# Tail keys and last queries as 64-row matmuls, one double bank for both heads' outputs, and FFN on two banks

## The chip, the core and the metric

The kernel runs on one core of a Trainium2 chip. The metric is the device time of one execution in microseconds (us); the kernel before has a median of 394.3 us over 3 runs (393.31 to 398.42). A separate execution was recorded by the hardware profiler, and every time of a single instruction comes from that one. Engines are named as in the profile: PE (TensorE, matmuls) with PEld (its weight loads), DVE (VectorE), ACT (ScalarE), POOL (GpSimd) and SP (SyncE, which issues DMAs). PE writes its results to PSUM, eight banks of 512 fp32 values per partition.

## The reference

Attention with a relative-position bias over 8 batches, 8 heads, 576 positions and 64 dimensions, then a feed-forward network (FFN) on the 4608 tokens that come out:

```python
scores = scale * np.matmul(q, k.transpose(0, 1, 3, 2))
bias = bias_table[bucket]            # bucket depends on |i - j| alone, constant from 128 on
scores = scores + bias.transpose(2, 0, 1)[None, :, :, :]
attn = np.exp(scores - np.max(scores, axis=-1, keepdims=True))
attn = attn / (np.sum(attn, axis=-1, keepdims=True) + 1e-09)
x = np.matmul(attn, v)               # transposed and reshaped to 4608 x 512
h = x @ w_in                         # 512 -> 2048
g = np.maximum(0.01 * h, h)
out = g @ w_out                      # 2048 -> 512
```

## The kernel before

**Head pairs.** Work goes by head pair: 8 batches of 4 pairs make 32 items, and the main loop has 33 passes. Pass n computes the scores of pair n and the value product of pair n-1. The program writes the order of every engine out by hand; each engine executes its instructions in that order and waits only on semaphores.

**Scores.** For a pair, the transposed keys `kt` and queries `qt` hold head 0 in partitions 0 to 63 and head 1 in partitions 64 to 127. 576 = 4 x 128 + 64, so there are four blocks of 128 keys and a tail of 64 keys, and likewise 512 queries and a last 64. `qk_mm(n, u)` makes one piece of the scores, transposed (keys in partitions). For u = 0 to 3 it is a key block against the first 512 queries, one 64-row matmul for each head (L301). For u = 4 it is the four key blocks against the last 64 queries (L305): these are 128-row matmuls, for which `apart` (L278) has made a copy of the last queries of both heads, side by side, with the other head's rows zeroed. For u = 5 it is the tail keys of both heads, masked by `apart` in the same way, against all queries (L308, L309). Scores go to `ps_s`, two buffers of two banks each.

**Exp and bias.** ACT takes the exp of each piece into `at_` or `at4_` (L319, L321, L326). DVE multiplies the band near the diagonal by the exp of the bias (`band`, L344).

**Value product.** `av(n, e)` makes head e's output in `ps_o`, which has a single bank: for each of five blocks of queries, four matmuls over the key blocks (L357) and one over the tail keys (L359). The tail matmul has 128 rows, with the other head's half of `v4` set to zero. A column of ones beside v gives the row sum; DVE takes its reciprocal and multiplies into `opair` (L362, L363). `x_transposes` then turns `opair` into `xT`, on PE for the first pairs and the last one and by a DMA on SP for the others.

**Queries and keys.** `transpose_q` and `transpose_k` for pair n+1 run within pass n. For the first ten pairs PE transposes (L272), and a copy takes the result out of PSUM (L286 on ACT or DVE, L291 on DVE); later a DMA on SP turns them ahead of time, and DVE copies from `tu`.

**FFN pieces.** A tile of 512 tokens is 16 "in" pieces (`ffn_in`: four matmuls into one bank, then ACT's Prelu, L393 and L395) and 16 "out" pieces (`ffn_out`: four of the sixteen matmuls into one bank, L404, and after every fourth piece DVE's copy to `y`, L409, and a store on SP). There are nine tiles. `moe(k)` puts k pieces at its place in a pass; `choose` picks "in" or "out" from counters that the program keeps while it is built: a tile's "in" pieces may start once its tokens are `ready` and not more than two tiles are open. A pass has seven such places for eight pieces in all. What is left over runs in `moe_rest` behind the last pass. FFN pieces and PE's transposes share `ps_m`, three buffers of one bank. With `ps_s` (four) and `ps_o` (one) this fills the eight banks.

**Around it.** `spin` runs matmuls on a tile of zeros while the first loads arrive. Loads of q, k and v are issued on POOL; transposing DMAs and output stores on SP.

Of the kernel before, what the change touches and what calls it, by code (L numbers as in the profile page):

```python
# [37 lines left out]
def kernel(  # L38
# [17 lines left out]
    P = 128  # L56
# [23 lines left out]
    ps_m_pool = ctx.enter_context(tc.tile_pool(name="ps_m", bufs=3, space=bass.MemoryType.PSUM))  # L80
# [18 lines left out]
    v4 = [per.tile([P, n_pairs, 2, D + 1], BF16, name=f"v4_{i}") for i in range(NBUF)]  # L99
# [16 lines left out]
    def load_v_part(b, j):  # L116
        i = b % NBUF
        for c in ((0,), (1, 2), (3,))[j]:
            nc.gpsimd.dma_start(  # L119
                out=vn[i][:, c, :, 0:D],  # L120
                in_=v[b, :, c * P : (c + 1) * P, :].rearrange("h s d -> s h d"),
            )
        if j == 2:
            for e in range(2):
                nc.gpsimd.dma_start(
                    out=v4[i][e * SL : (e + 1) * SL, :, e, 0:D],
                    in_=v[b, e::2, NJ * P : S, :].rearrange("h s d -> s h d"),
                )

    def load_v(b, h0, h1, by_head):  # L130
        i = b % NBUF
        p0, p1 = h0 // 2, h1 // 2
        if by_head:
            for h in range(h0, h1):
                nc.gpsimd.dma_start(
                    out=vn[i][:, :, h, 0:D],
                    in_=v[b, h, 0 : NJ * P, :].rearrange("(c s) d -> s c d", s=P),
                )
        else:
            for c in range(NJ):  # L140
                nc.gpsimd.dma_start(
                    out=vn[i][:, c, h0:h1, 0:D],
                    in_=v[b, h0:h1, c * P : (c + 1) * P, :].rearrange("h s d -> s h d"),
                )
        for e in range(2):
            nc.gpsimd.dma_start(
                out=v4[i][e * SL : (e + 1) * SL, p0:p1, e, 0:D],
                in_=v[b, h0 + e : h1 : 2, NJ * P : S, :].rearrange("h s d -> s h d"),
            )

    def clear_v(eng, i):
        eng.memset(v4[i], 0.0)
        for e in range(2):
            eng.memset(v4[i][e * SL : (e + 1) * SL, :, e, D : D + 1], 1.0)
        eng.memset(vn[i][:, :, :, D : D + 1], 1.0)
# [110 lines left out]
    def turned_pair(n, j):  # L266
# [3 lines left out]
        ps = ps_m_pool.tile([P, 8 * P], BF16, name="ps_t", tag="m")  # L270
# [12 lines left out]
    def transpose_q(n):  # L283
        qt = qts[n] = qt_pool.tile([P, S + P], BF16, name="qt")
        copy = nc.scalar.copy if n <= n_pairs and n != 1 else nc.vector.tensor_copy
        copy(out=qt[:, 0:S].rearrange("p (r c) -> p r c", c=NC), in_=turned_pair(n, 0))  # L286
        apart(qt)
# [6 lines left out]
    def qk_mm(n, u):  # L294

        qt, kt = qts[n], kts[n]
        ps = ps_s_pool.tile([P, 2, 512], FP32, name="ps_s")
# [5 lines left out]
        elif u == NJ:  # L303
            for c in range(NJ):
                nc.tensor.matmul(ps[:, 0, c * P : (c + 1) * P], lhsT=kt[:, c * P : (c + 1) * P],  # L305
                                 rhs=qt[:, S : S + P], start=True, stop=True)
# [8 lines left out]
    def exp_band(n, u, ps):  # L315
        b, p = items[n]
# [3 lines left out]
        elif u == NJ:  # L320
            nc.scalar.activation(  # L321
                at[:, :, :, 512:S].rearrange("p e c i -> p c e i"),
                ps[:, 0, :].rearrange("p (c e i) -> p c e i", e=2, i=SL),
                AF.Exp, scale=scale)
        else:
            nc.scalar.activation(at4[:, 0:S], ps.rearrange("p e i -> p (e i)")[:, 0:S], AF.Exp, scale=scale)  # L326
        if n > 1:
            band(n, u)
# [16 lines left out]

    def av(n, e):
        b, p = items[n]
        i = b % NBUF
        at, at4 = at_[n % 2], at4_[n % 2]
        if e == 0:  # L350
            ops_[n] = op_pool.tile([P, NJ + 1, 2 * D], BF16, name="opair")
        opair = ops_[n]
        ps = ps_o_pool.tile([P, NJ + 1, D + 1], FP32, name="ps_o", tag="ps_o")
        for ic in range(NJ + 1):
            for c in range(NJ):
                o = (e * NJ + c) * S + ic * P
                nc.tensor.matmul(ps[:, ic, :], lhsT=at[:, o : o + P], rhs=vn[i][:, c, 2 * p + e, :],  # L357
                                 start=(c == 0), stop=False)
            nc.tensor.matmul(ps[:, ic, :], lhsT=at4[:, ic * P : (ic + 1) * P], rhs=v4[i][:, p, e, :],  # L359
                             start=False, stop=True)  # L360
# [24 lines left out]
    gts = {}  # L385

    def ffn_in(T):
        t0 = T * TT
        gt = gts[T] = gt_pool.tile([P, n_fc, TT], BF16, name="gt")
        for f in range(n_fc):  # L390
            pm = ps_m_pool.tile([P, TT], FP32, name="pm1", tag="m")
# [6 lines left out]
    def ffn_out(T):  # L398
        t0 = T * TT
        gt = gts.pop(T)  # L400
        for ts in range(TT // P):
            pm = ps_m_pool.tile([P, DM], FP32, name="pm2", tag="m")
# [14 lines left out]
    turn = 0  # L417
# [31 lines left out]
    def moe(n_pieces):  # L449
        nonlocal turn  # L450
        for _ in range(n_pieces):
            kind = choose()
            turn ^= 1

            if kind and not (kind == "out" and made["in"] == 1 and running["in"] is None and turn):
                piece(kind)

    def moe_rest():
        while (kind := choose()):
# [9 lines left out]
    pw = ps_o_pool.tile([P, 512], FP32, name="ps_w", tag="ps_o")  # L469

    def spin(k):
        for _ in range(k):
# [12 lines left out]
    for n in range(N + 1):  # L485
        live = n < N
        if live:
            b, p = items[n]
            if n == 0:
                load_w_in(0)  # L490
                load_v(1, 0, H, False)
                load_w_in(1)
                load_w_out(0)
                load_w_out(1)
            elif 0 < b < B - 1:
                if p < 2:
                    load_qk(b + 1, 4 * p, 4 * p + 4)
                if p > 0:
                    load_v_part(b + 1, p - 1)
            if n + 1 < N and not by_dma(n + 1):  # L500
                pair_rows(n + 1)
            if n + AHEAD < N and by_dma(n + AHEAD):
                pair_rows(n + AHEAD)
                turn_by_dma(n + AHEAD)
            ps_a, ps_b = qk_mm(n, 0), qk_mm(n, 1)
            exp_band(n, 0, ps_a)
        moe(1)
        if live:
            exp_band(n, 1, ps_b)
        if n > 1:  # L510
            av(n - 1, 0)
        if n + 1 < N:
            transpose_q(n + 1)
        if n < 2:
            spin(3)
        moe(1)
        if live:
            ps_a, ps_b = qk_mm(n, 2), qk_mm(n, 3)
            exp_band(n, 2, ps_a)
        moe(1)  # L520
        if n > 1 and x_by_dma(n - 2):
            finished(n - 2)
        if live:
            exp_band(n, 3, ps_b)
        if n > 1:
            av(n - 1, 1)
        if n + 1 < N:
            transpose_k(n + 1)
        if n == 0:
            spin(4)  # L530
        if n == 1:
            spin(3)
        moe(1)
        if live:
            ps_a, ps_b = qk_mm(n, 4), qk_mm(n, 5)
            exp_band(n, 4, ps_a)
        if n == 1:
            exp_band(1, 5, ps_b)

            bands(0)  # L540
            av(0, 0)
            av(0, 1)
        moe(1)
        if n > 0:
            x_transposes(n - 1)
            if not x_by_dma(n - 1):
                finished(n - 1)
        moe(1)
        if n == 1:
            bands(1)  # L550
        elif live:
            exp_band(n, 5, ps_b)
# [32 lines left out]
```

## Time and profile before

| what | value |
|---|---|
| timed runs, median (lowest to highest) | 394.3 us (393.31 to 398.42) |
| span of the profiled execution, first to last instruction | 435.3 us |
| granted TensorE clock in it | 0.852 |
| PE busy | 421.2 us, 97% of the span |
| PEld, DVE, ACT, POOL busy | 199.4, 209.3, 242.2, 69.0 us |
| first FFN matmul at | 41.53 us |

The profiled execution has no other time of its own than its span. It is longer than the timed runs, and its durations on PE go with the clock granted there. PE's busy time is modelled and counts overlapping matmuls once, so the distance between the starts of matmuls tells more than their printed lengths. A row of the timeline gives the start, the length in us, the engine, the line, the tiles written and read, and the number of instructions merged.

### The profile page before, as it was taken

What the parts mean: (1) busy time and instruction counts of PE and PEld (TensorE: products, weight loads), DVE (VectorE), ACT (ScalarE), POOL (GpSimd) and SP (SyncE); (2) the same over time, 40 slices, a digit from 0 to 9 for tenths busy, and PEclk for the clock granted to TensorE, in tenths of its full rate; (3) what the DMA queues carried; (4) which work ended last, traced back from release to release, by engine and by line L of the source; (5) the groups of instructions that cost most, each with busy time, mean ns of one, the idle gap of its engine ahead of it and who ended that gap; (6) DMA issues with size and microseconds to landing.
All of it is one profiled execution on the core that took longest, in us unless ns stands there. A gap on an engine that the chain in (4) does not pass through costs nothing.

```text
span 435.3 us, 8219 instructions
## 1 busy us (share of the span) xinstructions
PE 421.2 (97%) x3384; PEld 199.4 (46%) x3384; DVE 209.3 (48%) x551; ACT 242.2 (56%) x343; POOL 69.0 (16%) x100
## 2 busy tenths in 40 slices
PE   8777999999999999999999999999999999999996
PEld 3445555444444444444444444444444454444442
DVE  6588557764556455555555455545554320000111
ACT  4776776576645666476646764676457713354000
POOL 8834230420051002400060004000000000000000
PEclk9888888888888888888888888888888888888888
DMA  8999992999289714974399349522422010000111
GB/s 107 194 196 197 206 168 42 106 131 146 64 82 172 113 27 81 185 123 44 68 152 171 44 68 98 115 37 54 60 65 17 24 43 24 26 24 0 74 48 72
DMA packets 103613, 39.89 MB, mean 92 GB/s; under 512 B 82576, under 2 KB 97944, under 8 KB 103576
## 3 DMA queue, kind: packets, MB, share of 16 engines
q0 software_dynamic: 53664, 18.36, 40.5%
q1 hardware_dynamic: 49912, 21.02, 26.8%
q8 instruction: 26, 0.43, 0.4%
q14 instruction: 11, 0.09, 0.1%
HBM read 37.68 MB, written 9.45 MB: 108 GB/s over the span
## 4 chain that ended last, share of the span: by engine, by line
PE 91%; DVE 5%; ACT 2%; issue 1%; ACTq 0%
PE ps_o L357 9%; PE ps_s L301 7%; PE ps_o L359 2%; PE ps_w L473 2%; PE ps_s L305 2%; PE ps_s L308 2%; DVE opair L363 1%; DVE at_113 L344 1%; PE pm_2157 L404 1%; PE pm_4504 L404 1%; PE pm_3930 L404 1%; PE pm_1566 L404 1%; PE pm_3339 L404 1%; PE pm_2748 L404 1%; PE pm_3191 L404 1%
## 5 line engine op out<-in xcount | busy, mean ns | idle before, releaser
L393 PEld LDWEIGHTS <-w_in_sb 128*128 128x128 bf16 x576 | 55.9, 104 | 75.6 <-issue 8.3
L404 PEld LDWEIGHTS <-gt 128*128 128x128 bf16 x576 | 54.2, 104 | 78.1 <-issue 15.0
L319 ACT ACTIVATE at_114<-ps_s 128x1024 bf16<-128x1024 f32 x64 | 62.9, 1023 | 29.4 <-PE ps_s L301 29.2
L319 ACT ACTIVATE at_113<-ps_s 128x1024 bf16<-128x1024 f32 x64 | 62.6, 1022 | 14.3 <-PE ps_s L301 14.1
L344 DVE TENSOR_TENSOR at_114<-at_114,hk 128x512 bf16<-128x512 bf16 (+1 forms) x64 | 32.2, 506 | 38.4 <-ACT at_114 L319 30.1
L344 DVE TENSOR_TENSOR at_113<-at_113,hk 128x512 bf16<-128x512 bf16 (+1 forms) x64 | 32.0, 506 | 37.9 <-ACT at_113 L319 33.7
L357 PEld LDWEIGHTS <-at_114 128*128 128x128 bf16 x640 | 29.4, 100 | 12.9 <-DVE opair L363 3.1
L357 PEld LDWEIGHTS <-at_113 128*128 128x128 bf16 x640 | 28.9, 100 | 12.6 <-DVE opair L363 3.9
L363 DVE TENSOR_TENSOR opair<-ps_o,rcp 128x320 bf16<-128x320 f32 x64 | 31.5, 491 | 2.2
L119 POOL DMA_DIRECT2D vn_107<-in_v_dram x12 | 10.7, 907 | 99.0 <-PE ps_o L359 98.9
L119 POOL DMA_DIRECT2D vn_106<-in_v_dram x12 | 10.6, 892 | 83.9 <-PE ps_o L359 79.5
L301 PE MATMUL ps_s<-qt,kt_111 64*128 64x512 bf16 x128 | 21.4, 405 | 1.0 <-ACT at_113 L321 0.4
L301 PE MATMUL ps_s<-qt,kt_110 64*128 64x512 bf16 x128 | 21.1, 403 | 0.7 <-ACT at_113 L319 0.5
L362 DVE RECIPROCAL rcp<-ps_o 128x5 f32<-128x5 f32 x64 | 12.2, 190 | 17.0 <-PE ps_o L359 17.0
L357 PE MATMUL ps_o<-vn_106,at_114 128*128 128x65 bf16 x320 | 15.7, 198 | 2.2 <-DVE opair L363 1.5
L357 PE MATMUL ps_o<-vn_106,at_113 128*128 128x65 bf16 x320 | 15.5, 198 | 2.3 <-DVE opair L363 2.1
L359 PEld LDWEIGHTS <-at_1_116 128*128 128x128 bf16 x160 | 15.9, 99 | 0.0
L359 PEld LDWEIGHTS <-at_0_115 128*128 128x128 bf16 x160 | 15.9, 99 | 0.0
L357 PE MATMUL ps_o<-vn_107,at_114 128*128 128x65 bf16 x320 | 15.2, 198 | 0.3 <-DVE opair L363 0.3
L357 PE MATMUL ps_o<-vn_107,at_113 128*128 128x65 bf16 x320 | 15.2, 198 | 0.2 <-DVE opair L363 0.2
L321 ACT ACTIVATE at_113<-ps_s 128x512 bf16<-128x512 f32 x16 | 9.5, 595 | 10.4 <-PE ps_s L305 10.4
L286 DVE COPY qt<-tu 128x576 bf16<-128x576 bf16 x22 | 14.2, 647 | 0.0
(879 smaller groups left out, 824.0 us busy)
## 6 DMA issues: line engine op xcount, KB each, us to landing
out_dram<-y SPq DMA_DIRECT2D x36, 256.0 KB, 2.2
w_in_sb<-in_moe_w_in_dram POOLq DMA_DIRECT2D x2, 1024.0 KB, 13.7
vn_107<-in_v_dram POOLq DMA_DIRECT2D x16, 128.0 KB, 5.7
w_out_sb<-in_moe_w_out_dram POOLq DMA_DIRECT2D x2, 1024.0 KB, 16.4
qn_102<-in_q_dram POOLq DMA_DIRECT2D x6, 288.0 KB, 12.5
kn_104<-in_k_dram POOLq DMA_DIRECT2D x6, 288.0 KB, 14.4
qn_103<-in_q_dram POOLq DMA_DIRECT2D x6, 288.0 KB, 7.4
kn_105<-in_k_dram POOLq DMA_DIRECT2D x6, 288.0 KB, 9.5
```

Of the source, the lines that this page charges most:

```text
L119: nc.gpsimd.dma_start(out=vn[i][:, c, :, 0:D], in_=v[b, :, c * P : (c + 1) * P, :].rearrange("h s d -> s h d"),)
L286: copy(out=qt[:, 0:S].rearrange("p (r c) -> p r c", c=NC), in_=turned_pair(n, 0))
L301: nc.tensor.matmul(ps[:, e, :], lhsT=kt[r, u * P : (u + 1) * P], rhs=qt[r, 0:512], start=True, stop=True)
L319: nc.scalar.activation(at[:, :, u, 0:512], ps, AF.Exp, scale=scale)
L321: nc.scalar.activation(at[:, :, :, 512:S].rearrange("p e c i -> p c e i"), ps[:, 0, :].rearrange("p (c e i) -> p c e i", e=2, i=SL), AF.Ex ...
L344: nc.vector.tensor_tensor(out=o, in0=o, in1=m, op=ALU.mult)
L357: nc.tensor.matmul(ps[:, ic, :], lhsT=at[:, o : o + P], rhs=vn[i][:, c, 2 * p + e, :], start=(c == 0), stop=False)
L359: nc.tensor.matmul(ps[:, ic, :], lhsT=at4[:, ic * P : (ic + 1) * P], rhs=v4[i][:, p, e, :], start=False, stop=True)
L362: nc.vector.reciprocal(rcp, ps[:, :, D : D + 1])
L363: nc.vector.tensor_tensor(out=opair[:, :, e * D : (e + 1) * D], in0=ps[:, :, 0:D], in1=rcp.to_broadcast([P, NJ + 1, D]), op=ALU.mult)
L393: nc.tensor.matmul(pm, lhsT=w_in_sb[:, c, f * P : (f + 1) * P], rhs=xT[c][:, t0 : t0 + TT], start=(c == 0), stop=(c == n_cc - 1))
L404: nc.tensor.matmul(pm, lhsT=gt[:, f, ts * P : (ts + 1) * P], rhs=w_out_sb[:, f, :], start=(f == 0), stop=(f == n_fc - 1))
```

## The change

- The tail keys' value product becomes ten 64-row matmuls for a pair (`av_tails`): head e uses partitions 64e to 64e+63 of `at4_` and `v4`, and no zeroed half is needed. It stands directly behind the first score visit.
- The last queries' scores (u = 4) become eight 64-row matmuls, head e into its own bank, behind u = 2 and 3. Queries no longer need `apart`.
- `ps_o` becomes one buffer of two banks, one for each head. The buffer is shared in turn with the scores of u = 4 (`ps_q`) and with PE's transposes of pairs 5 to 9 (`ps_tt`, q and k in one tile).
- `ps_m` has two buffers. Behind the last pass (`rest`), FFN takes banks from all three pools.
- The pass is put in another order: u = 0, 1, tails and head 0's output together, an "in" piece, head 1's output, an "in" piece, u = 2, 3, 4, a block of four pieces of one kind with u = 5 in its middle, two "in" pieces. `moe` places "in" pieces only; "out" pieces have their place only in the block. The copies for pair n+1 stand behind u = 5 from pass 4 on.
- The first two passes are written out ahead of the loop.

```diff
-    ps_m_pool = ctx.enter_context(tc.tile_pool(name="ps_m", bufs=3, space=bass.MemoryType.PSUM))
+    ps_m_pool = ctx.enter_context(tc.tile_pool(name="ps_m", bufs=2, space=bass.MemoryType.PSUM))
...
-        ps = ps_m_pool.tile([P, 8 * P], BF16, name="ps_t", tag="m")
+        if n <= n_pairs:
+            ps = ps_m_pool.tile([P, 8 * P], BF16, name="ps_t", tag="m")
+        else:
+            if j == 0:
+                turned[n] = ps_o_pool.tile([P, 2, 8 * P], BF16, name="ps_tt", tag="o")
+            ps = turned[n][:, j, :]
...
+        if u == NJ:
+            ps = ps_o_pool.tile([P, 2, 512], FP32, name="ps_q", tag="o")
+            for c in range(NJ):
+                for e in range(2):
+                    r = slice(e * D, (e + 1) * D)
+                    nc.tensor.matmul(ps[:, e, c * SL : (c + 1) * SL], lhsT=kt[r, c * P : (c + 1) * P],
+                                     rhs=qt[r, 512:S], start=True, stop=True)
+            return ps
...
-        elif u == NJ:
-            for c in range(NJ):
-                nc.tensor.matmul(ps[:, 0, c * P : (c + 1) * P], lhsT=kt[:, c * P : (c + 1) * P],
-                                 rhs=qt[:, S : S + P], start=True, stop=True)
...
+    def av_tails(n):
...
+        ps = outs[n] = ps_o_pool.tile([P, 2, 512], FP32, name="ps_o", tag="o")
+        for ic in range(NJ + 1):
+            for e in range(2):
+                r = slice(e * SL, (e + 1) * SL)
+                nc.tensor.matmul(ps[:, e, ic * (D + 1) : (ic + 1) * (D + 1)],
+                                 lhsT=at4[r, ic * P : (ic + 1) * P], rhs=v4[b % NBUF][r, p, :],
+                                 start=(ic == 0), stop=False)
...
     def moe(n_pieces):
...
+            if can("in"):
+                piece("in")
+
+    def moe_block():
+
+        kind = "out" if can("out") else "in"
+        for i in range(4):
+            if can(kind):
+                piece(kind)
+            if i == 1:
+                yield
+        yield
...
+    for n in range(2, N + 1):
         live = n < N
+        early = n + 1 <= n_pairs
+        if x_by_dma(n - 2):
+            finished(n - 2)
         if live:
...
+            begin(n)
             ps_a, ps_b = qk_mm(n, 0), qk_mm(n, 1)
+            exp(n, 0, ps_a)
+            exp(n, 1, ps_b)
+        av_tails(n - 1)
+        av(n - 1, 0)
+        if live:
+            band(n, 0)
+        if early:
+            transpose_q(n + 1)
+        moe(1)
+        av(n - 1, 1)
+        if live:
+            band(n, 1)
+        if early:
+            transpose_k(n + 1)
         moe(1)
         if live:
...
+            ps_a, ps_b, ps_c = qk_mm(n, 2), qk_mm(n, 3), qk_mm(n, 4)
+            exp(n, 2, ps_a)
+            band(n, 2)
+            exp(n, 3, ps_b)
+            exp(n, 4, ps_c)
+            band(n, 4)
+        x_transposes(n - 1)
+        if not x_by_dma(n - 1):
+            finished(n - 1)
+        block = moe_block()
+        next(block)
+        if live:
+            ps_a = qk_mm(n, 5)
+            exp(n, 5, ps_a)
+            band(n, 5)
+        if n + 1 < N and not early:
             transpose_q(n + 1)
+            transpose_k(n + 1)
+        next(block)
         moe(2)
     moe_rest()
```

More of the change, by code (lines that the diff above doesn't have):

```diff
@@ L416 @@
     share = 0
-    turn = 0
     def can(kind):
@@ L543 @@
[L543 to L552, printed above, removed]
+            ps_a, ps_b, ps_c = qk_mm(n, 2), qk_mm(n, 3), qk_mm(n, 4)
+            exp(n, 2, ps_a)
+            band(n, 2)
+            exp(n, 3, ps_b)
+            exp(n, 4, ps_c)
+            band(n, 4)
+        x_transposes(n - 1)
+        if not x_by_dma(n - 1):
+            finished(n - 1)
```

147 lines of the change are left out of this document (64 added, 83 removed).

## The prediction

> **What bounds the kernel now.** The page comes first: engine sums and granted clock; then the view of cores, and of the timeline the first FFN matmul.
>
> ```profile
> span 435.3 us, 8219 instructions
> PE 421.2 (97%) x3384; PEld 199.4 (46%) x3384; DVE 209.3 (48%) x551; ACT 242.2 (56%) x343; POOL 69.0 (16%) x100
> PEclk9888888888888888888888888888888888888888
> core 0: 435.3 us, clock 0.852
> ...
> 41.53 0.40 PE L393 MATMUL pm_780<-xT_94,w_in_sb 128*128 128x512 bf16 x1
> ```
>
> TensorE (PE) is the bound: every microsecond it idles or spends lands in the end, while DVE and ACT are half used. The profiled execution ran at clock 0.852, and its span alone is 41.0 us over the timed median of 394.3, so the timed runs had a faster clock. FFN work begins 41.5 us in; scaling the 393.8 us behind it by 0.852 gives 335.5, with the 41.5 before it 377, which leaves 17 us around the span. So I take the timed runs to be at about full clock, do the sum at the profile's clock first, and then once more with TensorE's times multiplied by 0.852 and DVE's and ACT's left alone.
>
> Next, the timeline over one steady pass (a head pair), cut to its turning points.
>
> ```profile
> 199.43 0.67 PE L301 MATMUL ps_s<-qt,kt_111 64*128 64x512 bf16 x4
> 200.03 1.94 ACT L319 ACTIVATE at_114<-ps_s 128x1024 bf16<-128x1024 f32 x2
> 200.03 1.16 PE L404 MATMUL pm_2748<-w_out_sb,gt 128*128 128x512 bf16 x4
> 201.02 0.28 PE L357 MATMUL ps_o<-vn_106,at_113 128*128 128x65 bf16 x4
> 201.82 0.42 PE L393 MATMUL pm_2936<-xT_94,w_in_sb 128*128 128x512 bf16 x1
> 202.57 0.41 PE L393 MATMUL pm_2936<-xT_97,w_in_sb 128*128 128x512 bf16 x1
> 202.91 0.64 PE L301 MATMUL ps_s<-qt,kt_111 64*128 64x512 bf16 x4
> 203.10 0.64 DVE L286 COPY qt<-tu 128x576 bf16<-128x576 bf16 x1
> 203.48 0.42 PE L393 MATMUL pm_2950<-xT_94,w_in_sb 128*128 128x512 bf16 x1
> 205.26 0.20 PE L359 MATMUL ps_o<-v_0_108,at_0_115 128*128 128x65 bf16 x1
> 205.49 0.19 DVE L362 RECIPROCAL rcp<-ps_o 128x5 f32<-128x5 f32 x1 [0.37 <-PE ps_o L359]
> 205.72 0.49 DVE L363 TENSOR_TENSOR opair<-ps_o,rcp 128x320 bf16<-128x320 f32 x1
> 206.13 0.64 DVE L291 COPY kt_110<-tu 128x576 bf16<-128x576 bf16 x1
> 206.27 0.44 PE L305 MATMUL ps_s<-qt,kt_111 128*128 128x128 bf16 x4
> 206.55 0.41 PE L308 MATMUL ps_s<-qt,kt_111 128*128 128x512 bf16 x1
> 206.79 0.19 PE L309 MATMUL ps_s<-qt,kt_111 128*128 128x64 bf16 x1
> 206.80 0.23 DVE L278 TENSOR_TENSOR kt_110<-kt_110,own 128x128 bf16<-128x128 bf16 x1
> 206.82 1.17 PE L404 MATMUL pm_2748<-w_out_sb,gt 128*128 128x512 bf16 x4
> 206.99 0.59 ACT L321 ACTIVATE at_114<-ps_s 128x512 bf16<-128x512 f32 x1
> 208.03 0.69 DVE L409 COPY y<-pm_2748 128x512 f32<-128x512 f32 x1
> 209.53 0.65 ACT L326 ACTIVATE at_1_116<-ps_s 128x576 bf16<-128x576 f32 x1
> 210.21 0.26 DVE L344 TENSOR_TENSOR at_1_116<-at_1_116,hk_101 128x192 bf16<-128x192 bf16 x1 [1.49 <-ACT at_1_116 L326]
> 210.38 0.35 DVE L256 COPY pr<-qn_103 96x768 bf16<-96x768 bf16 x1
> 210.65 0.35 DVE L256 COPY pr<-kn_105 96x768 bf16<-96x768 bf16 x1
> 210.93 0.65 PE L301 MATMUL ps_s<-qt,kt_110 64*128 64x512 bf16 x4
> 211.03 0.60 ACT L395 ACTIVATE gt<-pm_3026 128x512 bf16<-128x512 f32 x1 [0.36 <-PE pm_3026 L393]
> 211.52 1.94 ACT L319 ACTIVATE at_113<-ps_s 128x1024 bf16<-128x1024 f32 x2
> ```
>
> From pass start to pass start is 199.43 to 210.93 = 11.50 us. A piece of four 512-column matmuls takes 1.00 (200.03 to 201.02); eight pieces make 8.0, attention 3.5. Twenty-five value matmuls take 0.80 (201.02 to 201.82), 0.032 each. A score visit occupies 0.66: the last piece matmul begins at 202.57, so the visit could begin at 202.82, and the next piece begins at 203.48. Its 4 matmuls of 512 columns run two at a time in 0.50; 0.09 passes on entry, 0.07 on exit. DVE operations that don't depend on each other start 0.08 sooner than the printed length (210.38, 210.65); ACT's 0.1 sooner (211.03, 211.52), an exp pair 0.92 apart.
>
> **What it saves.** Per pass, the ten tail matmuls (L359) cost 10 x 0.032 = 0.32, and the last queries' scores (L305) 206.27 to 206.55 = 0.28. As 64-row pairs that share the array like L301's, they would cost 5 x 0.032 = 0.16 and 4 x 0.031 = 0.125. The number of 64-row visits stays two a pass, so entry and exit are paid as before. Gain 0.31, say 0.30 x 30 passes = 9.0 us (7.7 at full clock). Bounds: no sharing gives 0.03 a pass, full sharing 0.31; no row shows 64-row matmuls this short. I take sharing, since the 512-column row shares fully. The Trainium skill (TensorE: Matmul & The Clock Gate, section "Wait — 56ns, not 53.3ns?") says that matmul starts never come closer than about 25 ns; by it tails and scores would cost 0.25 and 0.20, a gain of 0.15 and a sum about 5 us higher. No run here shows it yet. The dropped mask of q (L278, 0.23 on DVE) and memsets lie beside PE work and count nothing.
>
> **What it adds: waits of TensorE.** The changed program's order names them, and the rows price them. I number passes by head pair, E is where qk_mm(n,5) leaves PE.
>
> *Steady passes (9, 13 to 15, 17 to 30: eighteen).* Counting the pieces that the program's counters allow, they run in, in, two out, scores 5, two out, in, in. Five allocations on two banks mean that the last "in" always takes the bank of the out piece just finished, so it waits for L431's y copy. On DVE that copy now stands behind exp 5's band, the q copy, the k copy and its mask, all formerly spread over the pass. Chain from E: exp 5 starts 0.20 later and takes 0.65, band starts after 0.03 and clears DVE in 0.17, q copy 0.56, k copy 0.67, mask 0.15, y 0.68, signal 0.05: E + 3.15. PE has three pieces meanwhile: 3.01, a wait of 0.14; at full clock 2.57, a wait of 0.58. There ACT also lags: Prelu, exps 2, 3, 4 hold exp 5 back by 0.2, and opair(e0) costs about 0.1 (below). I take 0.68. Sum 18 x 0.14 = 2.5, or 12.2. Queued behind that waiting matmul is all of PE: the next pass's scores, hence exps.
>
> *Passes 4 to 8.* Both transposes share one ps_tt tile, and the program has the k transposes wait for the q copy, which stands behind exp 5 and its band. Rows for it, for early passes and for one wait that is new elsewhere:
>
> ```profile
> L272 PE MATMUL ps_t<-ident,pr 96*128 96x96 bf16 x120 | 8.6, 211 | 0.0
> 39.08 0.75 DVE L286 COPY qt<-ps_t 128x576 bf16<-128x576 bf16 x1
> PE ps_o L357 <- DVE opair L363: 4.1, 7, 0.8
> 69.05 0.67 PE L301 MATMUL ps_s<-qt,kt_111 64*128 64x512 bf16 x4
> 77.41 0.64 PE L301 MATMUL ps_s<-qt,kt_110 64*128 64x512 bf16 x4
> ```
>
> From E: 0.20 + 0.65 + 0.03 + 0.17 + 0.75 + 0.05 = 1.85, while six transposes fill 0.43 (8.6 / 120 x 6): 1.42 a pass, 7.1 in all; in passes 4 and 5 exp 5 also stands behind two Prelus, +1.0 each: 9.1. At full clock 9.6.
>
> *Passes 7, 8, 12.* No "in" piece exists there, and moe() may no longer fill with "out". So av(e1), which waits for opair(e0), has no cover: from the last matmul's start to opair's end is 205.26 to 206.21 = 0.95. Then qk_mm(n,4) waits for opair(e1): 0.95 less the visit's 0.6 = 0.35. Today such a pass has no idle to lose: 69.05 to 77.41 is 8.36, against 3.5 + 4.0 for four pieces + 0.86 of transposes. So 1.3 x 3 = 3.9, and 4.0. In the steady passes one "in" piece (1.00; 0.86) covers the first wait, just.
>
> *Passes 11, 16, 12.* After the two "in" pieces of the block in 11 and 16, T's sixteen are done and neither kind is allowed: nothing lies between scores 5 and the next pass, whose first weights wait for the k copy. Exp 5 stands behind two Prelus, E + 0.96; then 0.65 + 0.03 + 0.17 + 0.56 + 0.64 + 0.05: E + 3.06, twice: 6.1; pass 12 has two out pieces as cover and waits 0.3. 6.4, at full clock 7.5.
>
> *Pass 10* runs eight "in" pieces on two banks: the third of the block waits for a Prelu queued behind exps 2 to 4, 0.6, or 1.2.
>
> *Nothing counted*: passes 0 to 3 (bound by exps and DVE in both, +-1.5); the last FFN stretch, which has eight more pieces, less the pieces missing earlier, and five banks; the DMA transposes of x, now issued ahead of the y store on SP but needed at the pass's first piece; the loads on POOL, whose order stays.
>
> **The sum.** Profile's clock: -9.0 + 2.5 + 9.1 + 3.9 + 6.4 + 0.6 = +13.5, a span of 449. Full clock: -7.7 + 12.2 + 9.6 + 4.0 + 7.5 + 1.2 = +26.8, on 394.3: 421.1. The timed clock is inferred, and waits overlap a little, so I state 418.
>
> **Rivals.**
> - *Waits covered (faster).* ACT and DVE reach the copies before PE asks, in every pass: 394.3 - 7.7 = 387. For it: both are half idle. Against it: the copies depend on exp 5, whose scores PE itself issues late. It decides if qk_mm(n,5)'s chain ends under E + 2.6.
> - *Only the irregular passes lose.* If y is in time: 421.1 - 12.2 = 409. It holds if the timed clock is nearer 0.9 or the chain half a microsecond shorter.
> - *Half of it.* Irregular waits, too, come out at half, as PE idle now lets ACT catch up: 394.3 - 7.7 + 11 = 398, within 2%.
> - *The 64-row matmuls don't share.* The change doesn't do what it says: 0.03 instead of 0.30 a pass gives +7, 427. Against it: L301 shares.
>
> **How the numbers follow.** Forecast (411 to 424) 0.53; only irregular 0.17; half 0.11; no sharing 0.12; covered 0.07. Two per cent (386.4 to 402.2) is about what a measurement of this kernel tells from no change. The first, second and fourth are slower, 0.82; "half" and a little of its neighbours same, 0.11; "covered" faster, 0.07. The range reaches from "half" at 398 to no sharing with the larger waits, 431, leaving out "covered" and the tails.
>
> **What would show it.** In the changed profile: L359 and L304 pairs with starts 0.03 per pair (sharing) or 0.06; PE waiting for y L431 in eighteen passes; ps_tt L275 for qt L289 five times, over 1 us each; ps_o L370 for opair L374 most in passes 7, 8, 12; L311 weights for kt L293 at passes 12 and 17, some 3 us each; PE's share falling from 97% towards 94%. I am wrong if those waits are absent, or if the timed clock isn't the one inferred.

## The result: slower, and where the 37 us lie

The kernel after takes 430.88 us (429.64 to 433.06, 4 runs) against 393.81 us (392.68 to 398.42, 4 runs) of the kernel before: a ratio of 1.095, interval 1.090 to 1.100. The forecast was 418, most likely 411 to 424; 430.88 lies at the very end of its whole range, 398 to 431. The sign held, but the loss is 37 us where 24 were forecast. The page of the kernel after, in the lines that answer to those of before:

```profile
span 428.0 us, 8434 instructions
PE 376.7 (88%) x3458; PEld 191.6 (45%) x3512; DVE 200.2 (47%) x517; ACT 239.5 (56%) x343; POOL 67.8 (16%) x98
PEclk9959899999998999999999999999999999999999
```

This execution took 429.74 us, so 1.7 us lies around its span. The clock line is nearly full but for a 5 near 21 to 32 us and two dips to 8. To compare like with like, the kernel before was profiled again (experiment e1) and was granted the full clock:

```profile
span 391.0 us, 8219 instructions
PE 374.1 (96%) x3384; PEld 186.9 (48%) x3384; DVE 208.5 (53%) x551; ACT 242.1 (62%) x343; POOL 69.0 (18%) x100
PEclk9999999999999999999999999999999999999999
```

Between the two, the span grows by 37.0 and PE's busy time by 2.6 only: most of the loss is idle time of PE. The view of waits of the kernel after says for whom PE idled (total us, times, longest):

```profile
PE pm L415 <- DVE y L431: 9.4, 18, 0.8
PE ps_tt L275 <- DVE qt L289: 7.6, 5, 1.7
PE ps_s L311 <- DVE kt L293: 7.0, 3, 3.2
PE ps_o L370 <- DVE opair L374: 5.5, 7, 1.1
PE pm L415 <- ACT gt L417: 2.4, 2, 1.6
```

The first three are the prediction's waits with its counts: y 18 times, the q copy 5 times, the k copy 3 times. The whole list sums to 43.8 us; that of the kernel before, again at full clock, sums to 11.9, of which 5.0 were already waits of L357 for opair. One steady pass of the kernel after shows how the y wait comes about:

```profile
206.08 0.61 PE L311 MATMUL ps_s<-qt,kt 64*128 64x512 bf16 x4
...
212.81 0.68 ACT L330 ACTIVATE at<-ps_s 128x576 bf16<-128x576 f32 x1
...
213.69 0.64 DVE L289 COPY qt<-tu 128x576 bf16<-128x576 bf16 x1
214.25 0.64 DVE L293 COPY kt<-tu 128x576 bf16<-128x576 bf16 x1
214.93 0.23 DVE L281 TENSOR_TENSOR kt<-kt,own 128x128 bf16<-128x128 bf16 x1
215.07 0.68 DVE L431 COPY y<-pm 128x512 f32<-128x512 f32 x1
...
215.80 1.02 PE L415 MATMUL pm<-xT,w_in_sb 128*128 128x512 bf16 x4 [0.49 <-DVE y L431]
...
216.76 0.60 PE L311 MATMUL ps_s<-qt,kt 64*128 64x512 bf16 x4
```

Exp 5, q copy, k copy, its mask and then y stand in one line on DVE; PE gets its bank at 215.80, 0.49 us late, and the next pass starts behind that piece. The pass takes 216.76 - 206.08 = 10.68.

Pass starts set side by side, after against e1, give the account. Where the two kernels place different numbers of FFN pieces in a pass, each piece is allowed for at 0.863 us. "Forecast" is the prediction's own terms at full clock, with the gain of 0.26 taken from each pass.

| passes | forecast | measured |
|---|---|---|
| eighteen steady (9, 13-15, 17-30) | +7.6 | +7.6 |
| 4 to 8 | +11.0 | +13.6 |
| 10 | +0.9 | +0.8 |
| 11, 12, 16 | +8.0 | +9.0 |
| 0 to 3 | -0.8 | +5.2 |

Measured, this makes 36.2 of the 37.0; the rest lies behind the start of pass 31. The row of passes 0 to 3, for which the prediction counted no waits, holds the largest part of the miss. Windows from 18 us to the start of pass 4 show what it is made of (columns: length, busy us and count of PE, PEld, DVE, ACT and POOL, granted clock, DMA share, GB/s); first the kernel after, with a later window that is used below:

```profile
18.00:40.27 22.27, 15.52 (x226) 11.15 (x226) 14.28 (x39) 11.02 (x15) 9.97 (x13) 0.69 1.51 192
...
130.00:140.00 10.00, 5.66 (x75) 3.45 (x75) 5.53 (x15) 6.15 (x9) 3.10 (x4) 0.83 0.39 49
```

and the kernel before (e1):

```profile
18.00:35.11 17.11, 12.16 (x216) 8.10 (x213) 13.66 (x40) 11.36 (x15) 8.04 (x10) 1.00 1.68 187
```

About as many matmuls (226 against 216) kept PE busy for 15.52 instead of 12.16 us, at a clock of 0.69 instead of 1.00. That is 3.4 of the 5.2; the other 1.8 is idle time (6.75 against 4.95). The waits of PE in the same stretch sum to 7.1 against 4.5. Those of the kernel after:

```profile
PE ps_o L359 <- DVE at L346: 1.9, 2, 1.3
PE ps_o L370 <- DVE opair L374: 1.7, 3, 0.8
PE ps_o L359 <- ACT at L326: 1.0, 1, 1.0
PE ps_s L311 <- ACT at L324: 0.9, 2, 0.5
...
PE ps_s L311 <- ACT at L330: 0.6, 1, 0.6
```

and of e1:

```profile
PE ps_o L357 <- DVE opair L363: 2.4, 3, 0.8
...
PE ps_o L357 <- DVE at L344: 0.6, 2, 0.3
...
PE ps_s L301 <- ACT at L319: 0.3, 1, 0.3
```

The tails (L359), which now open the value product, wait for the last exps and bands of their pair: 2.9 against 0.6. Scores wait 1.2 us more for the exps to free `ps_s`. The wait for opair was there before. The lists count 2.6 more of waiting where the windows have 1.8 more of idle time, since matmuls overlap and their ends are modelled.

### The profile page after: what moved, and what is told of

Read it like the earlier page. It is cut to its first block, busy times and chain, and to the rows that moved or that the text cites. A ratio compares the mean times of both kernels' runs of the same rounds, so it can differ in the third digit from the quotient of the medians.

```text
span 428.0 us, 8434 instructions
## 1 busy us (share of the span) xinstructions
PE 376.7 (88%) x3458; PEld 191.6 (45%) x3512; DVE 200.2 (47%) x517; ACT 239.5 (56%) x343; POOL 67.8 (16%) x98
## 4 chain that ended last, share of the span: by engine, by line
PE 55%; DVE 20%; ACT 15%; issue 7%; DMA 1%; another core or an unknown queue 1%; ACTq 0%; POOL 0%; POOLq 0%
PE pm L415 21%; PE pm L426 15%; PE ps_o L370 11%; ACT at L324 8%; DVE at L346 5%; PE ps_s L311 5%; ACT at L330 3%; DVE opair L374 3%; DVE y L431 3%; DVE qt L289 3%; DVE kt L293 3%; ACT at L326 3%; DVE rcp L373 1%; PE ps_o L359 1%; ACT gt L417 1%
## 5 line engine op out<-in xcount | busy, mean ns | idle before, releaser
L415 PE MATMUL pm<-xT,w_in_sb 128*128 128x512 bf16 x546 | 138.4, 379 | 14.8 <-DVE y L431 9.4
L417 ACT ACTIVATE gt<-pm 128x512 bf16<-128x512 f32 x144 | 86.2, 602 | 114.6 <-PE pm L415 114.5
L324 ACT ACTIVATE at<-ps_s 128x1024 bf16<-128x1024 f32 x128 | 124.0, 1027 | 34.0 <-PE ps_s L311 34.0
L426 PE MATMUL pm<-w_out_sb,gt 128*128 128x512 bf16 x553 | 130.7, 380 | 1.9 <-issue 0.7
L346 DVE TENSOR_TENSOR at<-at,hk 128x768 bf16<-128x768 bf16 (+3 forms) x160 | 72.0, 454 | 66.1 <-ACT at L324 30.5
L415 PEld LDWEIGHTS <-w_in_sb 128*128 128x128 bf16 x576 | 52.5, 98 | 71.4 <-issue 19.3
L370 PE MATMUL ps_o<-vn,at 128*128 128x65 bf16 x1280 | 52.6, 198 | 5.5 <-DVE opair L374 5.5
L431 DVE COPY y<-pm 128x512 f32<-128x512 f32 x36 | 24.7, 687 | 69.1 <-PE pm L426 66.1
L370 PEld LDWEIGHTS <-at 128*128 128x128 bf16 x1280 | 47.3, 101 | 16.7 <-issue 11.9
L311 PE MATMUL ps_s<-qt,kt 64*128 64x512 bf16 x256 | 41.4, 396 | 10.3 <-DVE kt L293 7.0
L330 ACT ACTIVATE at<-ps_s 128x576 bf16<-128x576 f32 x32 | 21.8, 681 | 1.7 <-PE ps_s L315 1.6
L359 PEld LDWEIGHTS <-at 64*128 64x128 bf16 x320 | 9.5, 95 | 11.3 <-DVE at L346 2.5
L359 PE MATMUL ps_o<-v,at 64*128 64x65 bf16 x320 | 11.1, 193 | 3.0 <-DVE at L346 1.9
```

Of the source, the lines that this page charges most:

```text
L311: nc.tensor.matmul(ps[:, e, :], lhsT=kt[r, u * P : (u + 1) * P], rhs=qt[r, 0:512], start=True, stop=True)
L324: nc.scalar.activation(at[:, :, u, 0:512], ps, AF.Exp, scale=scale)
L346: nc.vector.tensor_tensor(out=o, in0=o, in1=m, op=ALU.mult)
L415: nc.tensor.matmul(pm, lhsT=w_in_sb[:, c, f * P : (f + 1) * P], rhs=xT[c][:, t0 : t0 + TT], start=(c == 0), stop=(c == n_cc - 1))
L417: nc.scalar.activation(gt[:, f, :], pm, AF.Prelu, bias=0.0, scale=1.0, alpha=0.01)
L426: nc.tensor.matmul(pm, lhsT=gt[:, f, ts * P : (ts + 1) * P], rhs=w_out_sb[:, f, :], start=(f == 0), stop=(f == n_fc - 1))
```

## The experiments

**e1: the kernel before once more**, to see it at the clock of the timed runs.

> The kernel before, unchanged, to see its passes at the clock of the timed runs. If the changed kernel's unexplained 10 us come from the baseline (TensorE's part does not shrink by 0.852 everywhere, because entry and exit of a score visit and the short matmuls are fixed times), a steady pass lasts 10.2 to 10.5 us here, over the 9.8 that scaling gives. If they come from the clock gate instead, a steady pass lasts about 9.8 and the granted clock stays at 1.00 from 20 to 50 us, where the changed kernel had stretches at 0.50.

It took 393.76 us (392.76 to 395.17, 10 runs), ratio 1.0005 (0.9988 to 1.0022), and its span at full clock is 391.0. So the prediction's inference that timed runs have nearly the full clock was right, but not the 377 + 17 that it built on it: a span that scaled throughout would be 377. Of its expectation a part of each case came true: the pass is longer than 9.8, and the clock stayed at 1.00 from 20 to 50 us, where the kernel after had stretches at 0.50. A steady pass in the timeline of e1:

```profile
193.62 0.61 PE L301 MATMUL ps_s<-qt,kt 64*128 64x512 bf16 x4
194.16 1.04 PE L404 MATMUL pm<-w_out_sb,gt 128*128 128x512 bf16 x4
195.03 0.28 PE L357 MATMUL ps_o<-vn,at 128*128 128x65 bf16 x4
...
195.78 1.03 PE L404 MATMUL pm<-w_out_sb,gt 128*128 128x512 bf16 x4
...
203.81 0.61 PE L301 MATMUL ps_s<-qt,kt 64*128 64x512 bf16 x4
```

It lasts 203.81 - 193.62 = 10.19 and not 11.50 x 0.852 = 9.80. The FFN pieces scale (0.863 against 1.00), but 25 value matmuls take 195.78 - 195.03 = 0.75, where scaling gives 0.68.

**e2 and e3: the copies earlier.** In e2 the q and k copies for the next pair return to the middle of the pass wherever a DMA turned them, so that DVE is free for y; e3 moves them in all passes, and drops `ps_tt`, so that PE's transposes use `ps_m` as before.

```diff
-        early = n + 1 <= n_pairs
+        early = n + 1 <= n_pairs or (n + 1 < N and by_dma(n + 1))      # e2
+        early = n + 1 < N                                              # e3
...
-        if n <= n_pairs:                                               # e3
             ps = ps_m_pool.tile([P, 8 * P], BF16, name="ps_t", tag="m")
-        else:
-            if j == 0:
-                turned[n] = ps_o_pool.tile([P, 2, 8 * P], BF16, name="ps_tt", tag="o")
-            ps = turned[n][:, j, :]
```

> Of the changed kernel, the q and k copies of the passes from 9 on stand in mid-pass again (behind the value products), so they are out of the way of the y copy and early for the next pass. Theory of the prediction: TensorE's waits for y (9.4 us) and for kt (7.0 us) go, and the time falls by 14 to 17 us, to 414 to 417. Rival, that DVE has no room in mid-pass and the copies push the output scalings instead: waits for opair grow and the time falls by under 6 us.

> As the run before it, and in passes 4 to 8 too: TensorE's transposes of q and k stand in mid-pass, in the FFN's banks, one tile each. Theory: the wait of the k transposes for the q copy (7.6 us) goes as well, 5 to 9 us more than the run before it, 407 to 411. Rival, that two FFN banks cannot hold the transposes beside the pieces: no gain over the run before it.

e2 took 413.78 us (412.68 to 415.02), ratio 1.052 (1.048 to 1.055): 17.1 us sooner than the kernel after, just over the 14 to 17 expected. Its list of waits has neither the y wait nor the 7.0 for the k copy, and waits for opair did not grow (5.5 to 4.7), so the rival falls. The transposes' wait is still there:

```profile
PE ps_tt L275 <- DVE qt L289: 7.1, 5, 1.7
PE ps_s L311 <- ACT at L330: 4.8, 5, 1.5
PE ps_o L370 <- DVE opair L374: 4.7, 6, 1.1
```

e3 took 404.64 us (403.83 to 405.26), ratio 1.029 (1.026 to 1.031): another 9.1, where 7.1 of waits went. It changes the place of the copies and the tile of the transposes at once; no run parts the two. Together the two edits give back 26.2 of the 37, about the sum of the three rows (24.0). Of the second row, 1.8 stood in the kernel after too; new are 1.5 each in passes 12 and 17, where PE, behind the copies now made early, waits for exp 5 (L330 of e2) to free `ps_s`.

e2 also settles whether the 64-row matmuls share the array. Its timeline at the visits:

```profile
212.36 0.61 PE L311 MATMUL ps_s<-qt,kt 64*128 64x512 bf16 x4
212.80 0.28 PE L304 MATMUL ps_q<-qt,kt 64*128 64x64 bf16 x8
213.01 1.90 PE L426 MATMUL pm<-w_out_sb,gt 128*128 128x512 bf16 x8
...
218.62 0.61 PE L311 MATMUL ps_s<-qt,kt 64*128 64x512 bf16 x4
219.06 0.32 PE L359 MATMUL ps_o<-v,at 64*128 64x65 bf16 x10
219.31 0.78 PE L370 MATMUL ps_o<-vn,at 128*128 128x65 bf16 x20
```

A visit with nothing added takes 194.16 - 193.62 = 0.54 in e1. With ten tails it takes 219.31 - 218.62 = 0.69, with eight last-query scores 213.01 - 212.36 = 0.65. So ten tails cost 0.15 (15 ns each) and eight scores 0.11 (14 ns each), against 10 x 0.030 = 0.30 and 0.22 before: a gain of 0.26 a pass. In e2's trace the two tails of a pair start 3 to 4 ns apart, and the pairs follow each other at 29 to 35 ns. The Trainium skill's rule (TensorE: Matmul & The Clock Gate, section "Wait — 56ns, not 53.3ns?") that starts never come closer than about 25 ns does not hold for such pairs.

**e7: the tails alone back to 128 rows.** On e3, the tail matmuls stay where they are, but run over 128 rows with the other head's half of `v4` zeroed. This isolates the gain that the change is named for.

```diff
-                r = slice(e * SL, (e + 1) * SL)
                 nc.tensor.matmul(ps[:, e, ic * (D + 1) : (ic + 1) * (D + 1)],
-                                 lhsT=at4[r, ic * P : (ic + 1) * P], rhs=v4[b % NBUF][r, p, :],
+                                 lhsT=at4[:, ic * P : (ic + 1) * P], rhs=v4[b % NBUF][:, p, e, :],
                                  start=(ic == 0), stop=False)
```

> On the same run: the tails as 128-row matmuls with the other head's half of v4 zeroed, at the same place. If the 64-row pairs share the array fully (a steady visit with ten tails is 0.15 us longer than one without), a steady pass grows by 0.15 us from 10.11 to 10.26, and the time by 4 to 5 us. If the pairs are bound by a floor of 25 ns a matmul, by 0.05 us a pass, 1.5 us in all.

```profile
208.46 0.61 PE L308 MATMUL ps_s<-qt,kt 64*128 64x512 bf16 x4
209.00 0.49 PE L355 MATMUL ps_o<-v,at 128*128 128x65 bf16 x10
209.32 0.77 PE L366 MATMUL ps_o<-vn,at 128*128 128x65 bf16 x20
...
218.74 0.60 PE L308 MATMUL ps_s<-qt,kt 64*128 64x512 bf16 x4
```

Ten tails take 0.32 here (209.00 to 209.32), and the pass, seen from e7's two starts, 10.28 against 10.12 in e3: the 0.15 of full sharing, not the 0.05 that a 25 ns floor would leave. The time was 406.97 us (405.06 to 407.84), only 2.3 above e3, where 30 passes of 0.16 make 4.8. The runs of e7 had a higher clock (0.982 to 0.998) than those of e3 (0.979 to 0.983), which may have paid for the rest; the next experiments are about the clock, and the two kernels are set side by side at one clock further down.

**e4 and e8: PE kept busy in the opening passes.** e4 puts matmuls on zeros (`spin`) into the waits of the first passes of the kernel after; e8 does the same to e3. If waits are what lets the clock fall, it should hold.

```diff
+    spin(3)
     av_tails(0)
     av(0, 0)
+    spin(2)
     av(0, 1)
+    spin(2)
...
+        if n < 4:
+            spin(3)
         av_tails(n - 1)
         av(n - 1, 0)
+        if n < 5:
+            spin(2)
...
         moe(1)
+        if n < 4:
+            spin(2)
```

> The changed kernel with matmuls on a tile of zeros put where TensorE waits in passes 1 to 4. If the granted clock of 0.50 from 20 to 34 us and around 45 us is what TensorE's idle time there brings, and costs time, the clock stays at 1.00 in both and the time falls by 2 to 4 us. If the opening passes are bound by exps and DVE whatever the clock is, the time stays within 1 us.

> On the same run: matmuls on a tile of zeros where TensorE waits in passes 1 to 4, to hold its clock. The run with spins on the changed kernel reached pass 6 2.4 us sooner but fell to the 0.50 clock for longer near pass 12. Here no pass near 12 has a wait that long, so if the clock is worth 2.4 us in the opening, the time falls by 2 to 3 us; if not, it stays within 1 us.

In e4 the clock held through the opening. Near 135 us, where the kernel after had half clock for 3.4 us, e4 had it for 6.8; windows as above:

```profile
18.00:38.59 20.59, 15.45 (x244) 9.23 (x244) 14.04 (x38) 10.60 (x15) 9.67 (x13) 1.00 1.58 193
...
130.00:140.00 10.00, 8.33 (x82) 4.74 (x83) 5.00 (x15) 5.02 (x6) 4.42 (x6) 0.66 0.62 69
```

Pass 4 starts 1.7 sooner than in the kernel after, but PE is as long busy as there (15.45), now with the added matmuls. The times are no better: 430.19 us (428.48 to 433.69) for e4, 404.07 (402.92 to 407.85) for e8, both within 1 us of the kernels they were made from. The profiled execution of e8 had a mean clock of 0.999. So filling the waits kept the clock of the opening in these two executions, and the added matmuls took about as much time as it gave. What the opening costs at full clock without them, e4 and e8 can't tell.

**e5 and e9: the order of the opening.** On e3. e5 puts the tails of pairs 0 to 3 behind each head's twenty value matmuls, so that the value product no longer starts by waiting for the bands. e9 issues the scores u = 2 and 3 and their exps between the two heads' outputs in passes up to 4.

```diff
+        if n <= 3:                                       # e5, in av_tails; tails follow in av
+            return
...
+        if n <= 4:                                       # e9
+            ps_a, ps_b = qk_mm(n, 2), qk_mm(n, 3)
+            exp(n, 2, ps_a)
+            exp(n, 3, ps_b)
         av(n - 1, 1)
```

> On the run with all copies in mid-pass (404.64 us): for the first four pairs the tail matmuls stand behind each head's other value matmuls instead of ahead of them, so that TensorE needs the tail band last, as in the kernel before. If putting the tails first is what lengthens the opening passes, the waits for the band of DVE (2.0 us) go and the time falls by 2 to 3 us. If the opening passes are set by the clock or by other waits, it stays within 1 us.

> On the run with all copies in mid-pass (404.64 us): in passes 2 to 4 the scores u = 2 and 3 and their exps stand between the two heads' outputs again, as in the kernel before, in place of behind both. Theory: the opening passes are chains, and the new order makes ACT wait for both outputs to be scaled before it gets exps 2 and 3; then passes 2 and 3 shorten by about 1 us each and pass 4 by some, 2 to 3 us in all. Rival, that the opening is set by the granted clock and the tail band: within 1 us.

e5: 405.18 us (402.94 to 406.52), no gain. Its wait for the bands (2.0 in e3's list) is gone and pass 2 starts at 22.96 against 24.16, but it then spends 17 us at half clock and begins pass 5 at 54.0 against 53.5. e9: 403.24 us (402.83 to 405.16), 1.4 below e3; pass 5 begins at 52.36. Neither edit alone gives the opening back. (In the kernel before, the first tail stands behind four value matmuls and not behind twenty, so e5 goes further than that order.)

**e6 and e11: one bank for each head.** On e3, `ps_o` and `ps_q` become two tiles of one bank each, with the exp of the last queries done once for each head. The number of banks is the same; only the ties between them go. e11 is the same kernel again, since the profiled execution of e6 took 2094.05 us and tells nothing of its passes.

```diff
-            ps = ps_o_pool.tile([P, 2, 512], FP32, name="ps_q", tag="o")
+            ps = [ps_o_pool.tile([P, 512], FP32, name=f"ps_q{e}", tag=f"o{e}") for e in range(2)]
...
-        ps = outs[n] = ps_o_pool.tile([P, 2, 512], FP32, name="ps_o", tag="o")
+        ps = outs[n] = [ps_o_pool.tile([P, 512], FP32, name=f"ps_o{e}", tag=f"o{e}") for e in range(2)]
```

> On the same run: the two heads' outputs are two tiles of one bank in place of one tile of two, and the exp of the last queries' scores is taken for each head by itself. If the one shared tile is what holds back head 1's matmuls until head 0's output is scaled, the waits for opair in passes 7, 8 and 12 go and the hidden 0.11 us of a steady pass too: 4 to 6 us less. If the second head waits for something else, or the extra exp delays ACT as much, no gain.

> The run with the heads' outputs as two tiles once more, for its profile: no wait of TensorE for opair in passes 7, 8 and 12, and a steady pass of 10.00 us in place of 10.11, if the shared tile is what made head 1 wait.

The other three runs of e6 took 398.71, 400.24 and 401.77 us, ratio 1.017 (1.012 to 1.023): by their median 4.4 less than e3. (The 401.0 that an expectation below names is the median with the execution of 2094.05.) e11, a single run, took 396.88 at a clock of 0.994, where e6's runs had 0.978 to 0.987. In the timeline of e11 the starts of pass 4 and of two steady passes, and the window up to pass 4:

```profile
35.78 0.39 PE L306 MATMUL ps_s<-qt,kt 64*128 64x512 bf16 x2 [0.51 <-ACT at L319]
...
192.33 0.61 PE L306 MATMUL ps_s<-qt,kt 64*128 64x512 bf16 x4
...
202.34 0.61 PE L306 MATMUL ps_s<-qt,kt 64*128 64x512 bf16 x4
```

```profile
18.00:35.78 17.78, 12.50 (x225) 9.13 (x225) 13.68 (x39) 10.81 (x16) 8.73 (x11) 0.90 1.64 187
```

Pass 4 starts 0.7 behind e1's instead of 5.2: PE is busy for 12.50 us, since the clock is 0.90 over the stretch. The waits there sum to 5.7. None of them is for opair any more on `ps_o`, where the kernel before had 2.4; those for exps and bands are still there. So e11 doesn't undo what the change did to the opening, it makes up for it with a wait that the kernel before has too, and with a clock that fell for less long. A steady pass is 202.34 - 192.33 = 10.01, 0.10 below e3 and 0.18 below the kernel before: the change's gain of 0.26, less 0.08 for which e11's list has no wait. The shared tile thus costs 0.10 in each steady pass. What keeps e11 above the kernel before are above all passes 5 (+1.8), 10 (+0.7), 12 (+2.8) and 17 (+1.5), which the steady passes' -0.18 do not pay. In passes 7 and 8 nothing is gained (8.2 us each in e3 and e11): against the expectation the wait for opair does not go there, it moves on to the scores of u = 4, and in pass 12 too, as e11's list has it:

```profile
PE ps_q L299 <- DVE opair L370: 3.9, 4, 1.1
```

**e10: e5, e6 and e9 in one kernel.**

> The heads' outputs as two tiles (401.0 us), with the scores between the outputs in passes 2 to 4 and the tails behind the other value matmuls for the first four pairs. If the parts of the opening hold each other up (each alone gives its gain to the clock or to the next wait), together they give 4 to 5 us, 396 to 397. If the opening's loss lies elsewhere, 400 to 401.

397.13 us (395.64 to 402.02, 8 runs), ratio 1.007 (1.004 to 1.010, without the run of 402.02): near the 396 to 397 of the theory, and still not under the kernel before. Three of the eight runs had a clock of 1.000: 395.98, 396.36 and 396.59 us. The profiled execution took 400.2; its clock was at 0.50 for 13.65 us from 24.0 us on. Its window from 18 us to pass 4:

```profile
18.00:39.29 21.29, 18.37 (x226) 11.93 (x227) 14.04 (x39) 12.09 (x20) 10.17 (x14) 0.68 1.54 193
```

The waits of PE there sum to 2.8 us only, less than the 4.5 of the kernel before, and yet pass 4 starts 4.2 later than in e1: passes 2 and 3 took 8.78 and 8.12, against 7.82 and 6.03 in e11. One program at two clocks thus gives the price of the clock without added matmuls: 13.65 us at 0.50 go with 3.6 to 4.2 us of time.

**e12: cover for the irregular passes.** On e6, "out" pieces may stand at any place of a pass, and from pass 9 on two pieces go between the exps of u = 2, 3 and 4.

```diff
+    def slot(prefer="in"):
+        scarce = made["in"] == 1 and running["in"] is None and not can("in")
+        if half():
+            piece("out")
+        elif prefer == "in" and can("in"):
+            piece("in")
+        elif can("out") and not (scarce and units["out"]):
+            units["out"] += 1
+            piece("out")
+        elif can("in"):
+            piece("in")
...
+            if between:                                  # 9 <= n < N
+                slot("out")
             exp(n, 3, ps_b)
+            if between:
+                slot("out")
             exp(n, 4, ps_c)
```

> An attempt at a version that beats both: the heads' outputs as two tiles and all copies in mid-pass; an out piece may stand in any place where no in piece is allowed (four in a row with no in piece between, since each holds one of two banks), and from pass 9 on the first two pieces of the block are issued between the exps, so that their Prelus do not queue behind exps 3 and 4. If passes 12 and 17 (2.8 and 1.5 us over what their pieces cost in the kernel before) and pass 10 (0.7 us) lose for want of pieces and for Prelus queued behind exps, the span falls by 4 to 5 us from 395, and the time comes to 390 to 392, at or just under the kernel before. If those passes are bound by exp 5 itself, 396 to 398.

408.97 us (405.98 to 412.8), ratio 1.035 (1.031 to 1.040): both theories missed. Passes with eight pieces of both kinds fell to 9.91 to 9.93, which is the kernel before's 10.19 less the whole 0.26. But FFN now runs ahead of its input. The first row of its list of waits, and from the timeline the DMA's issue on SP and the matmul that waits:

```profile
PE pm L411 <- DMA xT<-opair: 9.1, 4, 4.3
```

```profile
130.27 1.77 SPq L381 DMA_TRANSPOSE xT<-opair  x1
...
139.21 0.38 PE L411 MATMUL pm<-xT,w_in_sb 128*128 128x512 bf16 x1 [4.34 <-DMA xT<-opair]
```

The transpose is issued at 130.27, and the matmul that needs it could have begun at about 134.9: pass 13 lasts 16.1. Four such waits make 9.1 us. No version here beats the kernel before.

**The clock over all runs.** Each timed run has its mean granted clock beside it, and within one kernel the time mostly follows it: the kernel after 433.06 us at 0.964 and 429.64 at 0.980; e4 433.69 at 0.976 and 428.48 at 0.992; e10 400.2 at 0.983 and 396.59 at 1.000; the kernel before 394.11 at 0.987 and 392.76 at 1.000 (an exception is e12, 406.2 at 0.978 and 410.85 at 0.979). A line through the four runs of the kernel after reaches 424.8 at full clock, one through e1's ten 392.6. This is an extrapolation (no run of the kernel after was above 0.980), but by it about 5 of the 37 us are clock (e4's line reaches 426.2) and 32 are waits and order. By lines of their own, through four runs each, e3 would be at 399.1 and e7, whose runs had 0.982 to 0.998, at 405.5, a difference of 6.4: with the clock evened out, e7 loses no less than the 4.8 that its passes say.

## Why the prediction was wrong, and what in it was right

- **Sign, sharing and gain: right.** 64-row matmuls share the array; the gross gain is 0.26 a pass at full clock, as forecast (e2, e7). The rival without sharing falls; so does the price by the 25 ns rule of the Trainium skill (TensorE: Matmul & The Clock Gate, section "Wait — 56ns, not 53.3ns?"). That this rival, at 427, came nearer to 430.88 than the forecast is luck, for its mechanism did not occur.
- **The y wait: right in place and count, under-sized, and the match of the sum is luck.** There are eighteen waits, 9.4 us in the list. The +7.6 of the table equals the forecast only because pass 9 stands in it with -1.5: there the kernel before waits for opair (0.78) and for the DMA of x (1.02), and the kernel after does neither. The other seventeen passes lost 9.1 where 7.1 was forecast. Such a pass paid 0.77 before the gain is taken off, not 0.68: 0.50 of visible wait, 0.10 for the shared tile (e11) and about 0.17 that no list of waits names. The rivals "covered" and "only the irregular passes lose" fall with it, and "half" with the next two points.
- **The q copy (9.6 forecast, though its own terms give 9.4; 7.6 in the list) and the k copy (7.5, for which the working shown at the profile's clock gives 6.4; 7.0): right in place, a little over-sized.** Passes 4 and 5 paid 1.7 each and not 2.4. e2 and e3 gave back 26.2 when they removed these and y, so they are causes and not only labels.
- **opair in passes 7, 8 and 12 (4.0): right in place, but over-sized.** The rows give 3.5, and the kernel before already waited 0.52 in passes 7 and 8 (at 69.25 and 77.09 in e1), where the prediction had found "no idle to lose": 2.5 net.
- **Prelu in pass 10 (1.2):** 0.76 there; the other wait of that row, 1.59 in pass 5, had no term. It is a part of what passes 4 to 8 lost beyond their terms. A stretch of 3.41 us at a clock of 0.50 from 43.2 us on is another, and the rest is not priced here.
- **The step that failed: "Nothing counted: passes 0 to 3 (bound by exps and DVE in both, +-1.5)".** They lost 5.2. The step read "bound by exps and DVE" as "indifferent to order", and it left the clock at full by its form. By the windows, 1.8 of the 5.2 is more idle time of PE: its waits for exps and bands grew from 0.9 to 4.4 us, and e5 shows that 2.0 of them hang on the tails' place. The larger part, 3.4, is PE's own work at a clock of 0.69 against 1.00, and e10, one program at two clocks, confirms a price of that order. That the waits bring the clock down is made likely by e4 and e8, where matmuls put into them kept it; it is not shown that they alone do.
- **Pass 12 was under-sized:** +2.8 against 1.3 + 0.3 less the gain. The window from 130 to 140 us has the granted clock at 0.83, behind a wait of 3.2 us for the k copy.
- **The time around the span: wrong, at little cost.** 17 us was taken for it; 1.7 to 1.8 was measured (429.74 with 428.0; 392.76 with 391.0). The difference was in the pass: the short matmuls and the visits' entry and exit do not shrink in proportion, so a full-clock pass is 10.19 and not 9.80. The sum starts from the measured 394.3, so only the sizes of its terms were touched.
- **From 421 down to 418:** the deduction for overlapping waits went the wrong way, since the unpriced opening outweighed it.
- What stays open: why the clock falls in one execution and not in another. In the 3.41 us before the first fall PE was busy for 1.86 us in the kernel after, 1.72 in e3, 1.98 in e10 and 1.65 in e11. But e1 kept 1.00 over an equal stretch with 1.69 (84.22 to 87.64 us), and e10, which fell in its profiled execution, had 1.000 in three other runs.

## What to carry to other kernels

When two results share one multi-bank tile, ask in each stage what covers the evacuation of the first while the second waits; where nothing does, the second waits. Two tiles of the same banks part them, here for one more ACT instruction a pass. That gave 0.10 in each steady pass, but nothing in passes 7 and 8, where the wait moved on to the next user of the bank. When copies are moved to the end of a pass, write down the queue in front of the next bank's release on their engine: here a saving of 0.26 on PE was traded for 0.5 us of waiting behind two copies and a mask. And the opening passes need terms of their own, for there no FFN piece covers a wait, and the clock may fall besides; speeding up a pass also moves the moment when its DMA'd inputs must be there.

## What the runs showed of the hardware

- Paired 64-row matmuls of 64 and 65 columns cost 14 to 15 ns each, half of a 128-row one of the same width (30 to 32 ns); the two of a pair start 3 to 4 ns apart (e2).
- The granted clock fell to 0.50 without a long pause of PE: in the kernel after it was at 0.50 from 19.3 us for 13.65 us, although no single wait of PE around it was over 1.3 us. The Trainium skill (TensorE: Matmul & The Clock Gate, section "HAM oscillation — how this bites in real kernels") speaks of idle gaps over about 3.4 us. Here the fall at 19.3 us came behind several short ones, as the same page of the Trainium skill, section "A second HAM failure mode: psum-queue depth-cycling", describes for another kernel. The stretches at 0.50 inside the kernels were 3.41, 6.83, 10.24, 13.65 and 17.07 us, multiples of 3.41. In its profiled execution e1 kept 1.00 with 4.5 us of waits in the same passes.
- The same program had different clocks from run to run (e10: 0.976 to 1.000), and its time went with them. The profiled execution of the kernel before that the prediction had was granted 0.852 from end to end, and its span was 435.3; what lowered it, no run here shows.
